# An order by a list scheduler, with gelus in place in PSUM, for a long-convolution and expert-layer kernel

## The chip, the cores and the metric

The kernel runs on one core of a Trainium2 chip. The core has TensorE (PE, its weight loads shown as PEld), VectorE (DVE), ScalarE (ACT), GpSimd (POOL) and SyncE (SP), each with an instruction queue of its own that runs in order; SP only issues transfers here. Products are written to PSUM, eight banks of 128 x 512 words of 32 bits; DVE and ACT read and write PSUM, POOL and the transfers do not. The metric is the device time of one execution in microseconds, the median of the runs; lower is better.

## What is computed

A filter along the time axis by a real Fourier transform of 3008 points, for 8 batches of 256 channels, and then, for each of the 24064 tokens, two products with a gelu between them:

```python
X = np.fft.rfft(x, axis=1)                       # x: (8, 3008, 256)
y = np.fft.irfft(X * (filt_r + 1j * filt_i)[None], n=3008, axis=1)
h = y.reshape(8 * 3008, 256) @ w_in              # 256 -> 2048
g = h * (1.0 / (1.0 + np.exp(-1.702 * h)))
out = (g @ w_out).astype(np.float32)             # 2048 -> 256
```

## The kernel before

The transform is split into 64 x 47 points. `fft(b)` is the way into and out of the frequencies. Its first step takes six tiles of x (512 KB each), splits every half tile into a high part (ACT, line 406) and a rest (POOL, line 407), multiplies both with a table (three matmuls into one bank, `mm3`), splits the result again (lines 411, 412) and stores it in the scratch array a_d by four transfers per tile, issued by ACT (line 417). Its second step runs for i = 0 to 15: `forward` multiplies a piece of a_d, loaded into zy by POOL's queue (line 426), with a table, joins the halves (`halves`, a copy on ACT, line 393, and an addition on DVE, line 394), applies the filter (`product`, lines 384 to 386 on DVE, 387 on POOL) and splits the result (lines 457, 458); `backward` multiplies it back, joins halves, and stores pairs of results in b_d by ACT (line 473). `pair_signal` (lines 499 on) loads four pieces of b_d (br), does the last inverse step on PE (lines 493, 495) for two tiles of 512 tokens and forms sums and differences of them on DVE (line 544), split again by ACT and POOL (lines 537 to 547).

Numbers are 32 bits wide. Every factor is held as a high part and a rest in the matmul's own 32-bit format (F32R), so that one product is three matmuls.

From batch 1 on, the expert layer works on two tiles of tokens (t = 0, 1) and two blocks of 128 hidden features (f = 0, 1) together, by seven products in place of eight, whose combination leaves the four results c_f,t. One such round is a *cycle*: 21 matmuls of the first layer (`product_of`, line 756, weights wt from a ring of three slots that line 174 loads from w_1) and 24 of the second layer for the cycle before (`second_of`, line 778, weights from a second ring of three loaded from w_2). A batch is three u (pairs of tiles; the last pair has 512 and 448 tokens) of eight cycles: 24 cycles, and batches 1 to 7 make 168. In a cycle the bank pa gathers four products one after the other; after the first, second and third, ACT copies its state to SBUF (e, lines 814, 823, 827). pb and pg each have a product of their own and get a copy added by DVE (lines 817, 829, 838); the sum goes to SBUF (c_s), except that pg gets one more product after line 829 has read it. The gelu runs twice on ACT (line 763 to the high part gh, line 764 in full width to SBUF) and the rest gl is the difference of the two (line 765, on POOL for two of the four results and on DVE for the other two).

Four of the eight PSUM banks (ps_h) serve pa, pb, pg and all products of the fft and the inverse transform, and four (ps_o) the sums of the second layer. While batch b is in the expert layer, `tick` advances fft(b+1) in 48 steps over the first 82 of 96 quarter cycles. The order in each engine's queue, the buffers and the semaphores are set by the framework's scheduler with a timing model of its own. Batch 0 runs in another form of the same layer (`mlp`).

Of the kernel before, what the change touches and what calls it, by code (L numbers as in the profile page):

```python
# [142 lines left out]

@with_exitstack
def tile_kernel(
# [9 lines left out]
    nc = tc.nc  # L155
# [7 lines left out]
    def raw(name):  # L163
        return sb.tile([P, 4, D], F32, tag="raw", name=name, bufs=7)

    def half(name):
        return sb.tile([P, 2, D], F32R, tag="half", name=name, bufs=4)

# [227 lines left out]
    def fft(b):  # L396

        a_d = dram.tile([2, 48, 64, D], F32, tag="a_d", name=f"a_d{b}")
        for c in range(6):
            xr = raw(f"x_{b}_{c}")  # L400
            load_in(xr, x[b, c])
            ah, al = (sb.tile([P, 4, D], F32R, tag="raw", name=f"a{n}_{b}_{c}", bufs=7) for n in "hl")
            for u in range(2):
                xh, xl = half(f"xh_{b}_{c}_{u}"), half(f"xl_{b}_{c}_{u}")
                src = xr[:, 2 * u : 2 * u + 2, :]
                nc.scalar.copy(xh, src)  # L406
                nc.gpsimd.tensor_tensor(xl, src, xh.bitcast(F32), ALU.subtract)  # L407
                ps = ps_h.tile([P, 2, D], F32, tag="h", name=f"s1_{b}_{c}_{u}")
# [4 lines left out]
                yield  # L413
            for j in range(2):
                n = NH * j + 4 * c
                for k, a in enumerate((ah, al)):
                    nc.scalar.dma_start(
                        a_d[k, n : n + 4].rearrange("n k d -> k n d"), a[64 * j : 64 * j + 64].bitcast(F32)
                    )
# [15 lines left out]
        def second(i, m, src, name):  # L435

            ps = [ps_h.tile([P, 2, D], F32, tag="h", name=f"{name}_{b}_{i}_{k}") for k in range(2)]
# [26 lines left out]
        def backward(i):  # L464
            g, u = divmod(i, 2)
            if u == 0:
                bes[g] = raw(f"b_{b}_{g}")
            ps = second(i, 2, zy[0][:Q, 2 + i % 2], "i2")
            halves(ps, bes[g][:Q, 2 * u : 2 * u + 2, :])
            if u == 1:  # L470
                be = bes.pop(g)
                for k in range(2):
                    nc.scalar.dma_start(b_d[:, 32 * k + 4 * g : 32 * k + 4 * g + 4, :], be[64 * k : 64 * k + 48])
# [5 lines left out]
        for i in range(2):  # L479
            yield  # L480
        for i in range(17):
            if i < 16:
                forward(i)
                yield
            if i:
                backward(i - 1)
                yield
# [26 lines left out]
    def pair_signal(b, u, ops):  # L514
# [10 lines left out]
        for k, t in enumerate((2 * u, 2 * u + 1)):  # L525
# [5 lines left out]
            for m in range(2):  # L531
                ps = ps_h.tile([P, 512], F32, tag="h", name=f"i1_{b}_{t}_{m}")
# [17 lines left out]
    def finish(pos, w, at, name):  # L550

        o = sb.tile([P, 2, 512], F32, tag="out", name=name)
# [173 lines left out]

    wa = const.tile([P, 4096], F32R, tag="wi_0", name="wa")
    wb = const.tile([P, 4096], F32R, tag="wi_1", name="wb")
    wc = const.tile([P, 4096], F32R, tag="wo_0", name="wc")
    c_f = const.tile([P, 2, 512], F32, tag="tab", name="c_f")  # L730
    ring_1 = [a.rearrange("p (h a c) -> p h a c", h=2, a=7) for a in (wa[:, 0:1792], wa[:, 1792:3584], wb[:, 0:1792])]
    ring_2 = [wc[:, 1024 * i : 1024 * i + 1024].rearrange("p (i h d) -> p i h d", i=2, h=2) for i in range(3)]
    g_h = [wb[:, 2048 + 512 * i : 2560 + 512 * i] for i in range(2)] + [wc[:, 3072:3584]]
    g_l = [wb[:, 3072 + 512 * i : 3584 + 512 * i] for i in range(2)] + [wc[:, 3584:4096]]
    g_h += [sb.tile([P, 512], F32R, tag="gh", name=f"ph{i}") for i in range(2)]
    g_l += [sb.tile([P, 512], F32R, tag="gl", name=f"pl{i}") for i in range(2)]
    c_s = [c_f[:, i] for i in range(2)] + [sb.tile([P, 512], F32, tag="g", name=f"pc{i}") for i in range(2)]
    turn = {"h": 0, "l": 0, "c": 0}
# [5 lines left out]
    def load_1(c):  # L744
        load_in(ring_1[c % 3].bitcast(F32), w_1[c % CYCLES])

    def load_2(c):
        load_in(ring_2[c % 3].bitcast(F32), w_2[c % CYCLES])

    def temp(name):  # L750
        return sb.tile([P, 2, D], F32, tag="half", name=name, bufs=4).rearrange("p a d -> p (a d)")

    def product_of(ps, c, a, y, w, first):
        wt = ring_1[c % 3]
# [5 lines left out]
    def gelu(src, w, cs, on):  # L760
# [3 lines left out]
        nc.scalar.activation(cs[:, :w], src[:, :w], AF.Gelu_apprx_sigmoid)  # L764
        on.tensor_tensor(gl[:, :w], cs[:, :w], gh[:, :w].bitcast(F32), ALU.subtract)  # L765
        return gh, gl

    def second_of(z, k):
# [5 lines left out]
        gp, w, wt = gs[f, t], ws[t], ring_2[c % 3]  # L774
        first, last = c % CYCLES == 0 and k < 2, c % CYCLES == CYCLES - 1 and k > 1
        for n, (wk, gk) in enumerate(((0, 0), (1, 0), (0, 1))):
            for m in range(2):
# [3 lines left out]
                )  # L781
# [102 lines left out]
```

## Time and profile before

| | us |
|---|---|
| median of 3 runs (lowest, highest) | 2706.75 (2699.62, 2708.13) |
| the profiled execution | 2708.51 |
| its span, first to last instruction | 2706.6 |

Busy time in that span: PE 2447.3 us (90%), PEld 1910.5 (71%), DVE 1845.9 (68%), ACT 1638.6 (61%), POOL 1478.1 (55%). The granted clock of PE has a mean of 0.967. Time runs through batch 0 to 437 us, batches 1 to 7 start at about 437, 765, 1098, 1436, 1771, 2108 and 2446 us, counted by the first copy of line 814 in each. In the views by stretch the columns are the stretch, its length, the busy time of PE, PEld, DVE, ACT and POOL with the number of instructions, the granted clock, the DMA share and GB/s. In the rows below times are microseconds unless marked ns; "<-" before a name says what ended a wait; a tile is named without its buffer number. Matmuls overlap, so PE's busy time counts the stretches in which at least one of them is under way.

### The profile page before, as it was taken

The page shows a single profiled execution, that of the slowest core. Times are in us where ns is not written, and L with a number is a line of the kernel's source. Part 1 is how long each engine was busy: PE and PEld are TensorE (multiplying, and loading weights), DVE is VectorE, ACT ScalarE, POOL GpSimd, SP SyncE. Part 2 cuts the span into 40 slices and gives each one's busy share as a digit, 9 for nine tenths or more (in the row PEclk, how much of TensorE's full clock was granted, in tenths as well). Part 3 has the DMA queues.
Part 4 walks back from the last instruction along what each step waited for, and adds up shares of the span by engine and source line. Part 5 has one row for each costly group of instructions (what it writes and reads, how often), then busy time and mean ns, then how long its engine had stood idle before and what let it go on. Part 6 is the DMA issues. An engine that isn't in the chain of part 4 may idle for free. (4 is left out here: it accounts for less than half of the span.)

```text
span 2706.6 us, 32274 instructions
## 1 busy us (share of the span) xinstructions
PE 2447.3 (90%) x10578; PEld 1910.5 (71%) x10578; DVE 1845.9 (68%) x2435; ACT 1638.6 (61%) x2937; POOL 1478.1 (55%) x1149
## 2 busy tenths in 40 slices
PE   7898899888998889989899898998889989899999
PEld 6666678666776667766677666776667766678887
DVE  6767984488745886559865598645886459965443
ACT  5555555566655666656666566655666656666665
POOL 3654643477545774447645476544774447754232
PEclk9899999899999999989999999999999989999999
DMA  9454446686667856668566676676866667655443
GB/s 264 146 159 124 122 116 205 175 209 181 201 217 191 214 169 206 224 179 214 160 202 229 179 209 179 187 226 179 210 180 190 222 181 207 187 174 170 158 146 106
DMA packets 199191, 500.49 MB, mean 185 GB/s; under 512 B 21488, under 2 KB 94448, under 8 KB 199024
## 3 DMA queue, kind: packets, MB, share of 16 engines
q1 hardware_dynamic: 120640, 387.50, 46.5%
q0 software_dynamic: 25088, 44.05, 8.6%
q10 hardware_dynamic: 53296, 66.86, 8.4%
q8 instruction: 85, 1.39, 0.2%
q14 instruction: 82, 0.67, 0.1%
HBM read 392.95 MB, written 105.38 MB: 184 GB/s over the span
## 5 line engine op out<-in xcount | busy, mean ns | idle before, releaser
L778 PE MATMUL o<-wb,wc 128*128 128x512 f32 (+1 forms) x1620 | 443.1, 397 | 31.1 <-POOL wb L765 16.1
L458 POOL TENSOR_TENSOR zy<-c_buf,zy 48x512 fp32r<-48x512 f32 x224 | 333.3, 1488 | 92.4 <-DVE zy L457 80.8
L778 PEld LDWEIGHTS o<-wb,wc 128*128 128x128 f32 x1620 | 303.6, 191 | 111.0 <-POOL wb L765 23.5
L387 POOL TENSOR_TENSOR c_buf<-c_buf,u_buf 112x512 f32<-112x512 f32 x128 | 187.7, 1466 | 241.0 <-DVE c_buf L386 240.6
L778 PE MATMUL o<-ph,wc 128*128 128x512 f32 (+1 forms) x1072 | 296.4, 396 | 5.4 <-ACT ph L763 3.9
L829 DVE TENSOR_TENSOR c_f<-g,e 128x512 f32<-128x512 f32 (+1 forms) x168 | 112.2, 668 | 260.7 <-ACT e L827 235.5
L765 POOL TENSOR_TENSOR wb<-c_f,wb 128x512 fp32r<-128x512 f32 (+1 forms) x135 | 179.2, 1327 | 188.3 <-ACT c_f L764 109.5
L765 POOL TENSOR_TENSOR pl<-c_f,ph 128x512 fp32r<-128x512 f32 (+1 forms) x135 | 181.5, 1345 | 178.9 <-ACT c_f L764 92.9
L778 PEld LDWEIGHTS o<-ph,wc 128*128 128x128 f32 x1072 | 203.8, 192 | 53.3 <-ACT ph L763 11.4
L778 PE MATMUL o<-wc 128*128 128x512 f32 (+1 forms) x804 | 226.1, 398 | 10.5 <-POOL wc L765 6.1
L764 ACT ACTIVATE c_f<-c_f 128x512 f32<-128x512 f32 x336 | 208.2, 623 | 14.7 <-DMA br<-b_d 7.0
L426 POOL DMA_DIRECT2D zy<-a_d x224 | 128.7, 576 | 140.6 <-DMA a_d<-al 66.3
L827 ACT COPY e<-a 128x512 f32<-128x512 f32 (+1 forms) x168 | 95.5, 569 | 154.8 <-PE a L756 153.3
L778 PE MATMUL o<-pl,wc 128*128 128x512 f32 (+1 forms) x536 | 170.9, 397 | 19.1 <-POOL pl L765 11.2
L778 PEld LDWEIGHTS o<-wc 128*128 128x128 f32 x804 | 151.8, 192 | 49.4 <-POOL wc L765 9.9
L838 DVE TENSOR_TENSOR pc<-g,e 128x512 f32<-128x512 f32 x168 | 115.6, 688 | 99.3 <-PE g L756 96.7
L394 DVE TENSOR_TENSOR c_buf<-s,c_buf 48x512 f32<-48x512 f32 x224 | 154.0, 687 | 34.7 <-ACT c_buf L393 30.1
L394 DVE TENSOR_TENSOR b<-i,b 48x512 f32<-48x512 f32 x224 | 153.9, 687 | 27.2 <-ACT b L393 22.1
L407 POOL TENSOR_TENSOR xl<-x,xh 128x512 fp32r<-128x512 f32 x84 | 114.6, 1365 | 103.0 <-ACT xh L406 81.1
L765 DVE TENSOR_TENSOR wb<-pc,wb 128x512 fp32r<-128x512 f32 (+1 forms) x135 | 126.3, 936 | 60.0 <-ACT pc L764 59.2
L457 DVE CAST zy<-c_buf 48x512 fp32r<-48x512 f32 x224 | 144.0, 643 | 26.0 <-POOL c_buf L387 21.6
L765 DVE TENSOR_TENSOR pl<-pc,ph 128x512 fp32r<-128x512 f32 (+1 forms) x133 | 121.9, 917 | 57.9 <-ACT pc L764 57.0
(172 smaller groups left out, 5904.1 us busy)
## 6 DMA issues: line engine op xcount, KB each, us to landing
wa<-w SPq DMA_DIRECT2D x112, 896.0 KB, 5.7
wc<-w SPq DMA_DIRECT2D x168, 512.0 KB, 3.5
wb<-w SPq DMA_DIRECT2D x56, 896.0 KB, 6.2
f_buf<-fs SPq DMA_DIRECT2D x224, 192.0 KB, 3.8
zy<-a_d POOLq DMA_DIRECT2D x224, 192.0 KB, 4.5
x<-in_x_dram SPq DMA_DIRECT2D x48, 512.0 KB, 4.3
a_d<-ah ACTq DMA_DIRECT2D x84, 256.0 KB, 4.3
a_d<-al ACTq DMA_DIRECT2D x84, 256.0 KB, 4.6
```

Of the source, the lines that this page charges most:

```text
L387: nc.gpsimd.tensor_tensor(u1, u1, u2, ALU.add)
L394: nc.vector.tensor_tensor(dst[h], ps[k][h], dst[h], ALU.add)
L407: nc.gpsimd.tensor_tensor(xl, src, xh.bitcast(F32), ALU.subtract)
L426: nc.gpsimd.dma_start(zy[0][64 * k : 64 * k + 48, i % 2].rearrange("p k s d -> p k (s d)"), src.rearrange("n k s d -> n k (s d)"),)
L457: nc.vector.tensor_copy(y[h, k], u1[h])
L458: nc.gpsimd.tensor_tensor(y[o, k], u1[h], y[h, k].bitcast(F32), ALU.subtract)
L764: nc.scalar.activation(cs[:, :w], src[:, :w], AF.Gelu_apprx_sigmoid)
L765: on.tensor_tensor(gl[:, :w], cs[:, :w], gh[:, :w].bitcast(F32), ALU.subtract)
L778: nc.tensor.matmul(pos[t][m][:, :w], wt[:, f, wk, P * m : P * m + P], gp[gk][:, :w], start=first and n == 0, stop=last and n == 2,)
L827: nc.scalar.copy(e[3][:, :w1], pa[:, :w1])
L829: nc.vector.tensor_tensor(cs[:, :w1], pg[:, :w1], e[3][:, :w1], ALU.add)
L838: nc.vector.tensor_tensor(cs, pg, e[2], ALU.add)
```

## The change

From batch 1 on the kernel no longer leaves the order to the framework. Engine calls are recorded with a price each (`Planner.add`, `price`), with the accesses that they depend on; then `plan` runs a list schedule over them and issues them in the order of its start times, under the framework's manual mode. A matmul's due time is its place in program order on PE, other steps are due as late as those that need them allow; each engine takes the ready step with the earliest due time, PE nothing that is due more than 30 us later than its head. The schedule also picks the slot of each temporary tile and the PSUM bank, holds SBUF-only steps of DVE and all steps of POOL apart, and prices a transfer by its size in one shared pipe. Besides the order:

- The additions of pb and of the second pg are written to the PSUM bank itself, and the second gelu is written over its source (PSUM for three of the four results); the difference reads it there. POOL takes one difference of four, DVE three. The first addition of pg still goes to SBUF.
- Rings of w_1 and w_2 have two slots instead of three, and gh and gl four instead of five each. The load of w_1 for cycle c+1 is recorded at the start of cycle c, that of w_2 for cycle c in cycle c.
- Ten buffers of 4 KB per partition are split into pools: two for x, four for the split results and b, four for the rest (there were seven in one pool). x is loaded one tile further ahead.
- All transfers go through SP: the stores of a_d and b_d from ACT, the loads of zy from POOL.
- The fft's parts are paced by PE's time (weights at the `yield`s) so that they end 36 us ahead of the batch's end. Batch 0's stores are all issued ahead of the new part.

```diff
+    def price(self, eng, call, args, aps):
...
+            return (0.6 if eng == "gpsimd" else 0.4), 3.2 + whole / 280e3, False
...
+                return (n + 32) / 2400, 0.1, False
...
+            return 0.18 + n * (0.8e-3 if any(spaces) else 0.88e-3), 0.0, False
...
+                return 0.15 + n * 1.06e-3, 0.0, False
+            fast = call in ("tensor_copy", "memset")
+            return 0.15 + n * (0.54e-3 if fast else 1.06e-3), 0.0, True
+        return 0.15 + n * 2.25e-3, 0.0, True
...
+                elif eng == "tensor" and target[n] > here + self.REACH:
+                    pass
+                else:
+                    key = (target[n] if eng == "tensor" else o.due, n)
+                    if (best is None or key < best[0]) and room(o, t):
...
+        store = nc.sync if nc.on else nc.scalar
...
-                nc.gpsimd.dma_start(
-                    zy[0][64 * k : 64 * k + 48, i % 2].rearrange("p k s d -> p k (s d)"),
+                (nc.sync if nc.on else nc.gpsimd).dma_start(
+                    zy[0][64 * k : 64 * k + 48, i % 2].rearrange("p k s d -> p k (s d)").bitcast(F32 if nc.on else F32R),
...
+    while stores:
+        store()
+    ctx.enter_context(tc.manual_schedule())
+    nc.on = True
...
+    ring_1 = [wa[:, 1792 * i : 1792 * i + 1792].rearrange("p (h a c) -> p h a c", h=2, a=7) for i in range(2)]
+    ring_2 = [wc[:, 1024 * i : 1024 * i + 1024].rearrange("p (i h d) -> p i h d", i=2, h=2) for i in range(2)]
...
+    for name, i, j in (("x", 0, 2), ("ab", 2, 6), ("raw", 6, 10)):
+        nc.pool(name, raws[i:j])
...
-        nc.scalar.activation(cs[:, :w], src[:, :w], AF.Gelu_apprx_sigmoid)
-        on.tensor_tensor(gl[:, :w], cs[:, :w], gh[:, :w].bitcast(F32), ALU.subtract)
+        nc.scalar.activation(src[:, :w], src[:, :w], AF.Gelu_apprx_sigmoid)
+        on.tensor_tensor(gl[:, :w], src[:, :w], gh[:, :w].bitcast(F32), ALU.subtract)
...
+    SPAN = 3 * CYCLES * 45 * 544 / 2400
+    TAIL, PARTS = 36.0, 6.0 + 12 * 1.5 + 2 * 5.0 + 32 * 3.3
...
-        if c + 2 < len(cycles):
-            load_1(c + 2)
-        if c == 0:
-            load_2(0)
         if c + 1 < len(cycles):
-            load_2(c + 1)
+            load_1(c + 1)
+        load_2(c)
...
-                cs = of(c_s, "c")
-                nc.vector.tensor_tensor(cs, pb, e[1], ALU.add)
-                gs[0, 0] = gelu(cs, 512, cs, nc.gpsimd)
+                nc.vector.tensor_tensor(pb, pb, e, ALU.add)
...
+            if k == 0:
+                gs[0, 0] = gelu(pb, 512, nc.vector)
             if k == 3:
                 product_of(pg, c, 2, t4, 512, False)
-                cs = of(c_s, "c")
-                nc.vector.tensor_tensor(cs, pg, e[2], ALU.add)
-                gs[1, 0] = gelu(cs, 512, cs, nc.vector)
+                nc.vector.tensor_tensor(pg, pg, e2, ALU.add)
+                gs[1, 0] = gelu(pg, 512, nc.vector)
```

## Rows read from the trace of the kernel before

**Rows 1.** Batches 3, 7: length, engines busy (count), clock, DMA share, GB/s.

```profile
1098.20:1436.40 338.20, 304.98 (x1280) 233.70 (x1280) 237.04 (x306) 208.42 (x372) 195.02 (x154) 0.96 0.68 196
...
2445.70:2706.60 260.90, 254.67 (x1164) 213.72 (x1164) 112.75 (x148) 159.19 (x287) 84.38 (x59) 1.00 0.43 143
```

**Rows 2.** The same columns in four stretches of batch 3.

```profile
1098.20:1224.50 126.30, 111.58 (x455) 85.40 (x456) 64.16 (x83) 73.22 (x134) 59.47 (x47) 0.93 0.69 207
...
1224.50:1343.30 118.80, 104.45 (x422) 76.24 (x422) 105.59 (x135) 75.32 (x131) 83.09 (x70) 0.97 0.70 187
...
1343.30:1436.40 93.10, 88.95 (x405) 72.07 (x403) 67.28 (x90) 59.88 (x110) 52.46 (x39) 1.00 0.62 192
...
1210.70:1251.70 41.00, 34.62 (x136) 23.60 (x135) 38.65 (x51) 26.80 (x48) 27.62 (x24) 1.00 0.86 211
```

**Rows 3.** The chain that ended last: start us, us, what.

```profile
2600.95 2.27 PE o L778 x10
...
2611.15 2.27 PE o L778 x10
...
2649.77 1.37 PE g L756 x6
...
2659.56 1.37 PE g L756 x6
```

**Rows 4.** Order of time, PE: start us, us, engine, line, operation, count.

```profile
465.83 1.05 PE L493 MATMUL i<-t_sb,br 128*128 128x128 f32 x8
```

**Rows 5.** Waits in batch 3: waiter <- releaser, us in all, times, longest.

```profile
DVE c_f L829 <- ACT e L827: 33.0, 8, 9.1
...
PEld g L756 <- DVE c_f L829: 13.7, 10, 3.8
```

**Rows 6.** Waits of SP's own queue over the whole span, same columns.

```profile
SPq L174 <- PE o L778: 708.4, 121, 14.3
```

**Rows 7.** Groups by line: count, busy us, mean ns, idle before.

```profile
L838 DVE TENSOR_TENSOR pc<-g,e 128x512 f32<-128x512 f32 x168 | 115.6, 688 | 99.3 <-PE g L756 96.7
...
L765 DVE TENSOR_TENSOR wb<-pc,wb 128x512 fp32r<-128x512 f32 (+1 forms) x135 | 126.3, 936 | 60.0 <-ACT pc L764 59.2
...
L544 DVE TENSOR_TENSOR t<-y,t 128x512 f32<-128x512 f32 x42 | 74.9, 1784 | 0.5
...
L764 ACT ACTIVATE pc<-pc 128x512 f32<-128x512 f32 x168 | 106.7, 635 | 6.3 <-DVE b L394 1.3 <-ACT wb L763 0.8 <-ACT ph L763 0.6
...
L764 ACT ACTIVATE pc<-a 128x512 f32<-128x512 f32 (+1 forms) x168 | 96.8, 576 | 0.0
```

**Rows 8.** One line's durations: ns min/median/max.

```profile
L544 DVE TENSOR_TENSOR t<-y,t x42: 678/1762/3240, 430.4 to 2578.5; 128x512 f32<-128x512 f32 x42
```

**Rows 9.** Order of time, ACT and its queue, in batch 3.

```profile
1130.90 2.11 ACTq L417 DMA_DIRECT2D a_d<-al  x2
...
1133.05 0.62 ACT L406 CAST xh<-x 128x512 fp32r<-128x512 f32 x1 [2.24 <-DMA a_d<-ah]
```

**Rows 10.** Batch 3: queues (packets, MB, share), issues (median us to landing).

```profile
q10 hardware_dynamic: 7552, 9.44, 9.7%
...
q0 software_dynamic: 3584, 6.29, 9.7%
...
wa<-w SPq DMA_DIRECT2D x16, 896.0 KB, 5.5
```

**Rows 11.** Issues in 1210 to 1250 us, same columns.

```profile
br<-b_d SPq DMA_DIRECT2D x4, 256.0 KB, 12.6
...
wb<-w SPq DMA_DIRECT2D x1, 896.0 KB, 10.5
```

**Rows 12.** Order of time around the start of batch 1.

```profile
433.40 0.86 PE L756 MATMUL a<-y_a,wa 128*128 128x512 f32 x3
...
436.96 0.58 ACT L814 COPY e<-a 128x512 f32<-128x512 f32 x1
...
441.50 0.58 SPq L600 DMA_DIRECT2D out_dram<-out  x1
```

More of the change, by code (lines that the diff above doesn't have):

```diff
@@ L144, in tile_kernel, with __init__, __getattr__, issue @@
+class Stream:
+    def __init__(self, planner, name, real):
+        self.planner, self.name, self.real = planner, name, real
+    def __getattr__(self, call):
+        real, planner = getattr(self.real, call), self.planner
+        def issue(*args, **kw):
+            if planner.on:
+                return planner.add(self.name, call, args, kw)
+            return real(*args, **kw)
+        return issue
 @with_exitstack
@@ L435, in second @@
         def second(i, m, src, name):
-            ps = [ps_h.tile([P, 2, D], F32, tag="h", name=f"{name}_{b}_{i}_{k}") for k in range(2)]
+            ps = [held(f"{name}_{b}_{i}_{k}") for k in range(2)]
             for k in range(2):
@@ L732, in tile_kernel @@
[L732 to L737, printed above, removed]
@@ L738, in tile_kernel, with fill @@
-    turn = {"h": 0, "l": 0, "c": 0}
+    def fill(tag, n, size, dtype, bufs):
+        return [sb.tile([P, size], dtype, tag=tag, name=f"{tag}_{i}", bufs=bufs) for i in range(n)]
+    ring_1 = [wa[:, 1792 * i : 1792 * i + 1792].rearrange("p (h a c) -> p h a c", h=2, a=7) for i in range(2)]
+    ring_2 = [wc[:, 1024 * i : 1024 * i + 1024].rearrange("p (i h d) -> p i h d", i=2, h=2) for i in range(2)]
+    g_h = [wc[:, 2048 + 512 * i : 2560 + 512 * i] for i in range(2)] + fill("gh", 2, 512, F32R, 2)
@@ new lines, in tile_kernel @@
+    g_l = [wc[:, 3072 + 512 * i : 3584 + 512 * i] for i in range(2)] + fill("gl", 2, 512, F32R, 2)
+    nc.pool("c", [c_f[:, i] for i in range(2)])
+    nc.pool("e", fill("g", 2, 512, F32, 2) + [wb[:, 3072 + 512 * i : 3584 + 512 * i] for i in range(2)])
+    raws = fill("raw", 7, 1024, F32, 7) + [wb[:, 1024 * i : 1024 * i + 1024] for i in range(3)]
+    for name, i, j in (("x", 0, 2), ("ab", 2, 6), ("raw", 6, 10)):
+        nc.pool(name, raws[i:j])
+    nc.pool("half", fill("half", 4, 512, F32R, 4) + [wa[:, 3584:4096]])
@@ L740, in of @@
+    nc.pool("out", fill("out", 2, 1024, F32, 2))
+    nc.pool("h", [ps_h.tile([P, 512], F32, tag="h", name=f"bank_h{i}") for i in range(4)])
+    nc.pool("o", [ps_o.tile([P, 512], F32, tag="o", name=f"bank_o{i}") for i in range(4)])
+    turn = {"h": 0, "l": 0}
     def of(ring, kind):
@@ L781, in second_of, with advance @@
                 )
+            advance(2 * (w + 32) / 2400)
         if last:
             finish(pos[t], w, at + 512 * t, f"{name}_{t}")
+    SPAN = 3 * CYCLES * 45 * 544 / 2400
+    TAIL, PARTS = 36.0, 6.0 + 12 * 1.5 + 2 * 5.0 + 32 * 3.3
+    clock, due, part = [0.0], [0.0], [iter(())]
+    def advance(us):
+        clock[0] += us
+        while due[0] <= clock[0]:
+            w = next(part[0], None)
+            due[0] = 1e9 if w is None else due[0] + w * (SPAN - TAIL) / PARTS
     prev, sig = None, None
     cycles = [(b, u, p) for b in range(1, B) for u in range(3) for p in range(CYCLES)]
-    for c in range(2):
-        load_1(c)
+    load_1(0)
     for c, (b, u, p) in enumerate(cycles):
         if u == 0 and p == 0:
-            next_batch(b, 0)
+            if b + 1 < B:
+                part[0], due[0] = fft(b + 1), clock[0]
         if p == 0:
@@ L794, in tile_kernel @@
             ws = (512, 512 if u < 2 else 448)
-            pos = [[ps_o.tile([P, 512], F32, tag="o", name=f"o_{b}_{u}_{t}_{m}") for m in range(2)] for t in range(2)]
+            pos = [
+                [nc.tile("o", (P, 512), F32, f"o_{b}_{u}_{t}_{m}") for m in range(2)]
+                for t in range(2)
+            ]
             y11, y21 = ([op["b"][:, h, m] for h in range(2)] for m in range(2))
@@ L855, in tile_kernel @@
     store()
+    nc.on = False
+    nc.plan()
 _OUTS = [((P, 2, B * S), "float32")]
```

311 lines of the change are left out of this document (270 added, 41 removed).

## The prediction

> **What bounds the kernel now.** I read the views in this order: the busy shares of a batch, of four stretches inside it, the chain that ended last, the waits, and the durations of the steps that the change touches.
>
> PE is busy for 305 of the 338.2 us of batch 3 [rows 1], but a busy PE is not a full one, so I price its work. In the last batch nothing but the mixture layer (products, gelus, second products; 24 cycles of 45 matmuls) and two inverse transforms runs. There the same point of a cycle returns after 10.20 us, 0.2267 us a matmul of 512 columns, or after 9.79 us in the third u, where a part is 448 wide [rows 3]. 16 x 10.20 + 8 x 9.79 = 241.5 us for the cycles of a batch. Batches 1 to 6 also carry the next batch's fft (96 matmuls of 0.2267 us are 21.8 us, 8 small ones at most 1 us) and the inverse transforms (96 records, of which 8 take 1.05 us [rows 4], 12 us). Sum: 276 us. Measured, batch 3 takes 338.2 us [rows 1], and the mean of batches 1 to 6 is 334.8 us, (2445.70 - 436.96)/6, from the first copy of batch 1 [rows 12] to the start of the last batch [rows 1]. So some 60 us in each of six batches are PE standing or at its lower clock: the granted clock is 0.96 there, a mix of its two levels, 1.2 and 2.4 GHz, and 1.00 in the last batch, where PE hardly stands [rows 1]. That batch has little left to win: 241.5 us, 24 second products of the batch before (5.4 us) and 64 inverse records (8.4 us) are 255 of its 260.9 us.
>
> Where do the 60 us lie? At 276/1280 = 0.2156 us for a mean matmul, batch 3's first 126.3 us hold 455 matmuls, 98 us of work (78%), the next 118.8 us hold 91 us (77%), the last 93.1 us hold 87 us (94%) [rows 2]. In the first stretch DVE and ACT are half idle: there the order stands in its own way, no engine does. In the middle DVE is tight, 38.65 of 41 us [rows 2]. The waits agree: DVE's largest is line 829's addition for the copy of line 827 (33.0 us), and PE's weight loads wait 13.7 us for that addition [rows 5]. It lies in a loop PE, ACT, DVE, PE, with 15 matmuls in program order between the product that starts it and the one that needs its bank, some 3.4 us, and each engine on the way has other work queued ahead.
>
> **The change part by part.** *The order.* It adds no work on PE and is worth what it takes back of the 60 us. I take the best that these rows show for a stretch with everything in it, 94%: 276/0.94 = 293 us a batch. Bounds: 276 us (nothing stands) and 335 us (nothing won). Gain: 6 x (335 - 293), about 250 us. DVE, ACT and the transfers have to fit into 293 us:
>
> *DVE.* The additions stay at about 0.69 us, that of line 838, which reads PSUM [rows 7]; written to PSUM they are in no row, and I take the same. A third subtraction per cycle comes over from POOL: 24 x 0.69 = +16.5 us a batch. The two that DVE has read SBUF twice and average 0.936 us [rows 7]; with the gelu in PSUM they should cost 0.69 as well: 48 x 0.25 = -12 us. DVE: 237 + 4.5, some 242 us of 293, 83%. Below that lies what collisions with POOL cost: line 544's subtraction in SBUF takes 1.784 us on average and 0.678 at the least [rows 7, 8], so six of them a batch give back up to 7 us if the order keeps them apart, and others like them more. Were the subtraction to stay at 0.936 us, DVE would have 260 us, 89%.
>
> *ACT.* The number of copies and gelus stays. A gelu in place (PSUM to PSUM) is in no row; the nearest are PSUM to SBUF, 0.576 us, and SBUF to SBUF, 0.635 [rows 7]. I take the first, since the source decides between these two: four of a cycle's eight gelus change, 24 x 4 x 0.055 = -5 us; at 0.635, nothing. 40 issues of transfers leave ACT's queue. Two of them took it 2.11 us, and ACT stood 2.24 us before its next step [rows 9]; six such groups a batch are 13 us. ACT: about 203 of 293, 69%.
>
> *All transfers from SP.* Per batch 24 stores of a_d, 16 of b_d and 32 loads of zy come to SP, 176 issues in all; at about 0.58 us [rows 12] that is 102 us of 293. Of the bytes, POOL's queue moved 6.29 MB in the engine time in which ACT's moved 9.44 MB, 9.7% of 338 us each [rows 10]; at ACT's rate they cost 22 instead of 33 us. The DMA share becomes (0.68 x 338 - 11)/293 = 75%. The price is order: all that is behind SP's head waits for what the head waits for, and SP stood up to 14.3 us for a buffer [rows 6], which a weight ring three deep covered. The ring becomes two deep: load c+1 starts when cycle c-1 is done and must land within cycle c, 10.2 us of PE time. Its median landing is 5.5 us [rows 10]; behind four loads of br, which took 12.6 us themselves, it was 10.5 us [rows 11]. So I count 0 in most cycles and 1 or 2 us near the three br bursts of a batch; these lie within the 6% that I leave.
>
> The Trainium skill, page "DMA: Bandwidth & Descriptors", section "Queues, rings and completion order", says that each DMA engine takes turns, packet by packet, between the queue rows that have work. This speaks against the change: a weight load on SP's row has its turn beside the bursts of ACT and POOL today, and in a single row it would stand behind them. No row separates the two; the 10.5 us are a load behind others of its own row, which agrees.
>
> *Additions and gelu in PSUM.* The banks of pb and pg are now held through two gelus and the subtraction, 0.6 + 0.6 + 0.69 = 1.9 us longer, that of pa by the subtraction, 0.7 us: 4.5 us more per cycle, on four banks shared with the fft. Bounds: 0 (another bank is free) and 4.5/4 = 1.1 us of PE per cycle. I take 0, since the second products, 24 of 45 matmuls, need none of these banks and can fill. The Trainium skill, page "PSUM — Partial Sum Buffer", section "Summary: rules for kernel authors", asks to evacuate PSUM promptly; by that, the third rival below is the outcome. No run here shows it yet.
>
> *The seam.* The new part's first weight load comes behind batch 0's last store on SP, issued at 441.50 us [rows 12]. With its 0.58 us, as much for the load and 5.5 us of landing, the first product starts near 448 us instead of 433.40, and the first copy near 450 instead of 436.96 [rows 12]: +13 us; 0 if the load is issued ahead of the store.
>
> *Sum*, against the profiled execution's span of 2706.6 us (the execution took 2708.5 us, the median of the three runs is 2706.75, so nothing is scaled): 437 + 13 + 6 x 293 + 260 (the last batch) = 2468 us.
>
> **The rivals.**
> 1. *Near the ideal.* 98%, 282 us a batch: 710 + 6 x 282 = 2402 us. For it: the last batch. Against: no stretch with an fft in it comes close.
> 2. *DVE is the bound of the middle.* The 118.8 us stretch has 8 cycles and 105.6 us of DVE [rows 2], of them 8 x (3 x 0.69 + 2 x 0.93) = 31 us the mixture's and 74 us the rest's. The change paces the fft's second half over about 15.5 instead of 14.1 cycles: 74 x 0.91 + 8 x 6 x 0.69 = 100 us, which at the 94% of the 41 us stretch take 107 us, where PE needs 90/0.94 = 96. 11 us over 8 cycles are some 17 us over the part that the easy ends of a batch don't absorb: 310 us, 2570 us. For it: those 94% are there today. Against: fewer collisions, and the fft may lag into the easy stretch.
> 3. *Banks.* The upper bound above, 24 x 1.1 = 27 us a batch: 320 us, 2630 us.
> 4. *Slower: weights late.* With a ring of two and one queue, the weight load stands at SP behind a store or a zy load that waits for DVE, and lands too late in most cycles. It decides from 710 + 6T > 2707 on, T = 333 us: 40 us over 293, 1.7 us in each cycle, an issue delay plus landing of more than 12 us every time. At 13.5 us T is 341 us and the time 2756 us. For it: 10.5 and 12.6 us [rows 11], SP's 14.3 us [rows 6]. Against: a median of 5.5 us leaves 4.7 us of slack.
> 5. *It doesn't do what it says.* Durations on the chip differ from those that the order was made with, and the engines wait as long in other places: T about 333 us, 2708 us.
>
> **How the numbers follow.** Forecast (T from 286 to 302 us) 0.49, near the ideal 0.12, DVE 0.19, banks 0.08, slower 0.09, no change 0.03. The predicted time is the forecast's. The range takes in the forecast, half of the ideal's cases and the DVE rival, and reaches to the banks: 2380 to 2625 us. A measurement of this kernel tells about 0.3%, 8 us, from no change: faster 0.88, same 0.03, slower 0.09.
>
> **What would show it.** Right: batches 1 to 6 of 286 to 302 us each, a clock of 0.99 or 1.00, DVE near 80% of a batch, its subtraction after a gelu at 0.69 us, no issue of transfers on ACT, PE's waits for DVE's addition below 5 us a batch, the first product of batch 1 near 448 us. DVE rival: middle stretches with DVE at 94%. Banks: PE's weight loads waiting for a subtraction or a gelu. Weights: PE waiting for the transfer of the weights. Wrong would be a mean batch over 325 us, or an in-place gelu far from 0.58 us.

## The result, and the profile after

| | us |
|---|---|
| changed kernel, median of 4 runs (lowest, highest) | 2451.99 (2448.9, 2453.48) |
| kernel before, median of 4 runs | 2704.55 |
| ratio, 95% interval | 0.9066, 0.9047 to 0.9084 |
| span of the profiled execution, before and after | 2706.6, 2447.1 |

The time fell by 9.3%; 2468 us were forecast. In the trace of the changed kernel nearly every line of the planned part is L393, the place where the plan issues its steps, so groups are told apart by tiles: bank_h is a bank of ps_h, bank_o one of ps_o. Batches are counted from the start of DVE's one addition into c_f per cycle (line 829 before), since that step is the same in all variants. By it batches 1 to 6 took (2453.4 - 443.1)/6 = 335.0 us before and (2194.2 - 440.0)/6 = 292.4 us after. Of the 259.5 us between the two spans, 3.1 lie ahead of batch 1, 256.1 in batches 1 to 6, and 0.3 in the last.

The views by stretch of the changed kernel (columns as in [rows 1]): batch 3, its cycles 0 to 7, 8 to 15 and 16 to 23, ten microseconds from its cycle 6, and the last batch:

```profile
1026.20:1320.20 294.00, 284.57 (x1282) 231.26 (x1281) 218.94 (x331) 204.30 (x370) 139.88 (x97) 0.99 0.75 225
...
1026.20:1134.50 108.30, 102.78 (x459) 83.08 (x458) 69.07 (x105) 73.23 (x134) 48.38 (x35) 0.98 0.84 253
...
1134.50:1231.20 96.70, 94.27 (x418) 74.76 (x417) 87.46 (x129) 70.94 (x127) 53.41 (x37) 1.00 0.71 213
...
1231.20:1320.20 89.00, 87.52 (x409) 73.41 (x408) 62.41 (x99) 60.13 (x111) 38.09 (x27) 1.00 0.69 206
...
1100.00:1110.00 10.00, 5.90 (x24) 4.06 (x23) 9.76 (x13) 4.74 (x9) 5.29 (x4) 0.97 0.64 164
...
2194.20:2447.10 252.90, 247.72 (x1136) 208.28 (x1134) 109.20 (x166) 150.49 (x275) 46.83 (x33) 0.99 0.42 148
```

Batch 3 is down from 338.2 us in [rows 1] to 294.0 us with the same 1280 matmuls (a few records at the edges aside) and the clock at 0.99. DVE's busy time fell from 237 to 219 us although it has 24 steps more; ACT's fell by 4 us, POOL's by 55. Of the 44.2 us that the batch lost, 23.8 are time in which PE did nothing (33.2 us before, 9.4 after), and 20.4 are PE's busy time, at a clock of 0.99 in place of 0.96. By the price of the prediction the three stretches are at 91%, 93% and 99%; those of [rows 2] were at 78%, 77% and 94%. More than half of what is left stands in one place, cycles 4 to 7: they take 54.5 us for 206 matmuls, 44.4 us of work by the same price, 10 of the batch's 18 us over it (the row stands under e10 and e11). In the fifth row, ten microseconds of that place, PE has 5.90 us and DVE 9.76.

What PE waits for in batch 3 of the changed kernel, the longest first (waiter, releaser, us in all, times, longest):

```profile
PEld bank_h L393 <- DVE c_f L393: 5.9, 4, 3.9
...
PE bank_h L393 <- DVE c_f L393: 4.5, 3, 3.5
...
PEld bank_h L393 <- DVE c_buf L393: 2.3, 6, 1.0
...
PEld bank_o L393 <- ACT wc L393: 2.0, 4, 0.9
```

The loop through the addition into c_f is still the largest wait, 5.9 us for the weight loads against 13.7 in [rows 5]; waits for a gelu or its difference are 2 us each or less, and nothing on PE waits for a transfer.

The chain through that place, in order of time (start us, us, what):

```profile
1104.93 1.68 DVE u_buf L393
...
1106.63 1.65 DVE u_buf L393
...
1108.34 0.57 issue
...
1108.91 0.69 DVE c_f L393
...
1109.65 2.07 PE bank_h L393 x5
```

The addition that PE needs (c_f) stands on DVE behind two products of the filter (u_buf) that take 1.68 and 1.65 us in place of 0.69, with POOL at work in SBUF beside them. Over the whole span, the 160 of these products that had no step of POOL beside them took at most 0.691 us, the 64 others up to 2.23.

Durations in the changed kernel over the whole span (ns min/median/max, first and last start):

```profile
L393 ACT ACTIVATE bank_h<-bank_h x504: 533/593/627, 438.2 to 2438.0; 128x512 f32<-128x512 f32 x168
...
L393 DVE TENSOR_TENSOR bank_h<-bank_h,g x224: 680/700/700, 436.0 to 2429.5; 128x512 f32<-128x512 f32 x112
...
L393 DVE TENSOR_TENSOR gl<-bank_h,gh x336: 606/691/694, 442.6 to 2438.6; 128x512 fp32r<-128x512 f32 x113, 128x448 fp32r<-128x448 f32 x55
```

The gelu in place takes 593 ns, the addition in place 700, the difference after it 691, with a maximum of 694.

Transfers of batch 3 of the changed kernel (queues, then issues with the median us to landing), to be read beside [rows 10], and the start of the planned part in order of time, beside [rows 12]:

```profile
q1 hardware_dynamic: 25857, 66.01, 74.8%
...
wa<-w SPq DMA_DIRECT2D x24, 896.0 KB, 7.5
...
zy<-a_d SPq DMA_DIRECT2D x32, 192.0 KB, 4.1
```

```profile
405.85 0.82 SPq L393 DMA_DIRECT2D wa<-w  x2
...
429.93 0.86 PE L393 MATMUL bank_h<-y_a,wa 128*128 128x512 f32 x3
...
437.81 0.58 SPq L406 DMA_DIRECT2D out_dram<-out  x1
```

All transfers of the kernel are on one queue now; the weights land after 7.5 us instead of 5.5. The first weights of batch 1 were issued at 405.85 us, 32 us ahead of batch 0's last store, and the first product started at 429.93 us.

### The profile page after: what moved, and what is told of

Its sections match the earlier page's. It is cut to its first block, busy times and chain, and to the rows that moved or that the text cites. A ratio compares the mean times of both kernels' runs of the same rounds, so it can differ in the third digit from the quotient of the medians.

```text
span 2447.1 us, 32185 instructions
## 1 busy us (share of the span) xinstructions
PE 2333.3 (95%) x10578; PEld 1897.0 (78%) x10578; DVE 1751.6 (72%) x2603; ACT 1615.3 (66%) x2937; POOL 1105.8 (45%) x789
## 4 chain that ended last, share of the span: by engine, by line
PE 76%; DVE 15%; DMA 3%; issue 2%; ACT 2%; POOL 1%; SPq 0%; ACTq 0%; DVEq 0%; POOLq 0%
PE bank_h L393 38%; PE bank_o L393 33%; PE h L406 2%; PE o L406 2%; DVE c_buf L393 1%; DVE u_buf L393 1%; DVE gl L406 1%; DVE wb L393 1%; DVE c_buf L406 1%; DVE u_buf L406 1%; DVE w_tu L406 1%; DVE bank_h L393 1%; DVE zy L393 1%; DVE ws L406 1%; DVE gl L393 1%
## 5 line engine op out<-in xcount | busy, mean ns | idle before, releaser
L393 PE MATMUL bank_o<-wc 128*128 128x512 f32 (+1 forms) x2016 | 553.8, 390 | 5.4 <-ACT wc L393 3.5
L393 PE MATMUL bank_h<-y_a,wa 128*128 128x512 f32 (+1 forms) x1584 | 434.9, 393 | 14.8 <-DVE c_f L393 8.8
L393 PEld LDWEIGHTS bank_o<-wc 128*128 128x128 f32 x2016 | 378.2, 189 | 91.0 <-ACT wc L393 10.6
L393 POOL TENSOR_TENSOR wc<-c_f,wc 128x512 fp32r<-128x512 f32 (+1 forms) x168 | 214.0, 1274 | 495.6 <-ACT c_f L393 366.5
L393 PE MATMUL bank_o<-gh,wc 128*128 128x512 f32 (+1 forms) x1344 | 390.2, 388 | 0.5 <-ACT gh L393 0.2
L393 PEld LDWEIGHTS bank_h<-y_a,wa 128*128 128x128 f32 x1584 | 294.0, 189 | 85.1 <-DVE c_f L393 11.8
L393 POOL TENSOR_TENSOR zy<-c_buf,zy 48x512 fp32r<-48x512 f32 x192 | 273.7, 1426 | 132.1 <-DVE zy L393 116.4
L393 DVE TENSOR_TENSOR gl<-bank_h,gh 128x512 fp32r<-128x512 f32 (+1 forms) x336 | 226.8, 677 | 114.5 <-ACT bank_h L393 109.4
L393 ACT ACTIVATE bank_h<-bank_h 128x512 f32<-128x512 f32 (+1 forms) x504 | 297.8, 591 | 0.0
L393 PEld LDWEIGHTS bank_o<-gh,wc 128*128 128x128 f32 x1344 | 251.8, 188 | 49.2 <-ACT gh L393 2.6
L393 ACT COPY wb<-bank_h 128x512 f32<-128x512 f32 (+1 forms) x309 | 178.6, 578 | 161.8 <-PE bank_h L393 159.3
L393 PE MATMUL bank_h<-y_bt,wa 128*128 128x512 f32 (+1 forms) x960 | 272.1, 393 | 13.3 <-DVE c_f L393 10.0
L393 POOL TENSOR_TENSOR c_buf<-c_buf,u_buf 112x512 f32<-112x512 f32 x96 | 125.1, 1303 | 285.4 <-DVE c_buf L393 273.1
L393 ACT ACTIVATE gh<-bank_h 128x512 fp32r<-128x512 f32 (+1 forms) x336 | 197.4, 588 | 67.2 <-DVE bank_h L393 37.6
L393 DVE TENSOR_TENSOR raw<-bank_h,raw 48x512 f32<-48x512 f32 (+1 forms) x264 | 180.8, 687 | 63.0 <-ACT raw L393 55.2
L393 DVE TENSOR_TENSOR bank_h<-bank_h,g 128x512 f32<-128x512 f32 x224 | 155.8, 696 | 93.3 <-PE bank_h L393 50.6
L393 PEld LDWEIGHTS bank_h<-y_bt,wa 128*128 128x128 f32 x960 | 177.9, 189 | 54.6 <-DVE c_f L393 13.5
L393 PE MATMUL bank_o<-gl,wc 128*128 128x512 f32 (+1 forms) x672 | 217.0, 387 | 0.0
L393 ACT COPY g<-bank_h 128x512 f32<-128x512 f32 x224 | 131.8, 588 | 111.0 <-PE bank_h L393 103.5
L393 DVE TENSOR_TENSOR wc<-bank_h,wc 128x512 fp32r<-128x512 f32 x168 | 115.7, 689 | 109.8 <-ACT bank_h L393 108.9
L393 DVE TENSOR_TENSOR c_f<-bank_h,wb 128x512 f32<-128x512 f32 (+1 forms) x168 | 112.2, 668 | 78.7 <-ACT wb L393 76.2
L393 PE MATMUL bank_h<-zy,de_sb 112*112 112x512 f32 (+1 forms) x408 | 154.6, 392 | 10.6 <-DVE wc L393 6.4
```

Of the source, the lines that this page charges most:

```text
L393: getattr(getattr(self.nc, o.eng), o.call)(*map(real, o.args), **{k: real(v) for k, v in o.kw.items()})
```

## The experiments

My theory: the order carries the gain; the gelus in place and the single queue each add little. The rivals give it to one of those two. A second question is what the remaining 18 us of batch 3 over the priced 276 are: late transfers, DVE as the bound, or the order itself. All ratios are to the kernel before on the same chip, by 3 rounds each.

| variant | median us | ratio (95%) | batch, us (mean of 1 to 6) |
|---|---|---|---|
| changed kernel | 2452.0 | 0.9066 (0.9047, 0.9084) | 292.4 |
| e3 order undone | 2689.0 | 0.9973 (0.9950, 0.9995) | 331.0 |
| e1 issuing undone | 2490.5 | 0.9240 (0.9215, 0.9264) | 299.2 |
| e2 in place undone | 2515.6 | 0.9332 (0.9307, 0.9357) | 303.1 |
| e7 before, all from SP | 2665.3 | 0.9897 (0.9877, 0.9918) | 328.3 |
| e8 before, in place | 2661.3 | 0.9836 (0.9786, 0.9887) | 327.6 |
| e9 another plan | 2460.9 | 0.9143 (0.9119, 0.9167) | 294.3 |
| e4 SBUF steps not kept apart | 2474.4 | 0.9179 (0.9149, 0.9209) | 297.0 |
| e5 few weights, planned anew | 2399.5 | 0.8908 (0.8890, 0.8926) | 283.9 |
| e6 less DVE, planned anew | 2397.8 | 0.8902 (0.8884, 0.8919) | 284.1 |
| e10 few weights, same plan | 2449.7 | 0.9054 (0.9011, 0.9097) | 292.4 |
| e11 less DVE, same plan | 2420.9 | 0.8946 (0.8896, 0.8997) | 287.4 |
| e12 the fft earlier and slower | 2401.7 | 0.8876 (0.8835, 0.8918) | 284.3 |

**e3, the order alone undone.**

```diff
-    ctx.enter_context(tc.manual_schedule())
```

> The changed kernel with its planner's choice of buffers, banks and recorded program, but the framework's own scheduler (as before the change) sets the order of each engine's queue. Theory (the order carries the gain): batches 1 to 6 go back from 294 to 330 us or more, time 2670 to 2800 us, and PE again waits for DVE's addition into c_f. Rival (gelus in place and transfers from SP carry it): at most 310 us a batch, 2450 to 2550 us.

The gain is gone: 0.9973, 331.0 us a batch. Its batch 3, and three of its waits there:

```profile
1103.90:1436.70 332.80, 301.07 (x1281) 233.01 (x1280) 230.02 (x331) 203.75 (x370) 139.61 (x97) 0.97 0.66 199
```

```profile
PEld bank_h L393 <- ACT wb L393: 8.2, 12, 2.7
...
PEld bank_h L393 <- DVE c_f L393: 6.8, 9, 4.1
...
PEld bank_o L393 <- ACT wc L393: 6.1, 5, 2.8
```

With the same steps, banks and queues as the changed kernel, 332.8 us instead of 294.0, and PE stands in many places for a few microseconds each, six kinds of wait of 5 to 8 us among its weight loads (three are shown), at a clock of 0.97. The theory's lower bound for a batch, 330 us, is met. The buffers here were chosen for another order, so 331 us is not what the old order does at its best; e7 and e8 bound that.

**e7 and e8, one other part alone, in the kernel before.**

```diff
-                    nc.scalar.dma_start(
+                    nc.sync.dma_start(
...
-                nc.gpsimd.dma_start(
+                nc.sync.dma_start(
...
-                    nc.scalar.dma_start(b_d
+                    nc.sync.dma_start(b_d
```

> The kernel before with one part of the change alone: all its transfers from SP, the order still the framework's. Theory (the order carries the gain, this part nothing by itself): 2660 to 2760 us. Rival (the stalls came from transfers issued on ACT): below 2620 us. Second rival (one queue makes the weights late): above 2780 us.

```diff
-                nc.vector.tensor_tensor(cs, pb, e[1], ALU.add)
-                gs[0, 0] = gelu(cs, 512, cs, nc.gpsimd)
+                nc.vector.tensor_tensor(pb, pb, e[1], ALU.add)
+                gs[0, 0] = gelu(pb, 512, pb, nc.vector)
...
-                gs[0, 1] = gelu(pa, w1, of(c_s, "c"), nc.vector)
+                gs[0, 1] = gelu(pa, w1, pa, nc.vector)
...
-                nc.vector.tensor_tensor(cs, pg, e[2], ALU.add)
-                gs[1, 0] = gelu(cs, 512, cs, nc.vector)
+                nc.vector.tensor_tensor(pg, pg, e[2], ALU.add)
+                gs[1, 0] = gelu(pg, 512, pg, nc.vector)
```

> The kernel before with one part of the change alone: additions and second gelus in place in PSUM, three of the four differences on DVE; order and issuing as before. Theory (the order carries the gain): the banks are held longer and the framework's order knows nothing of collisions, 2640 to 2740 us. Rival (in place carries the gain): below 2600 us. Rival on banks: above 2760 us.

Both lie within the times that the theory gave, though e7's theory gave its part nothing by itself, and both are a small gain: 1.0% for the queue, 1.6% for the gelus in place. In e9 below two plans with the same steps differ by 0.85%, so what each of the two is worth alone stays uncertain. Together with e3: without the new order none of the gain is left, so the order is worth most of the 9.3%, some 7% if the other two are taken off in full. No run has the new order with both other parts undone.

**e1 and e2, one other part undone, under the new order.**

```diff
-        store = nc.sync if nc.on else nc.scalar
+        store = nc.scalar
...
-                (nc.sync if nc.on else nc.gpsimd).dma_start(
+                nc.gpsimd.dma_start(
...
-                    (nc.sync if nc.on else nc.scalar).dma_start(b_d
+                    nc.scalar.dma_start(b_d
```

> Undoes one part: in the planned part the stores of a_d and b_d are issued by ACT again and the loads of zy by POOL. Theory (order carries the gain): the plan knows of the issues, ACT has 70% and POOL less than 50% of work, so 0 to 4 us a batch, 2450 to 2476 us. Rival (the queues were the stall): 10 us a batch or more, above 2510 us. Second rival (one queue delays the weights): faster, below 2440 us, and the weights' median landing falls from 7.5 us back towards 5.5 us.

299.2 us a batch, and 1.9% more time than the changed kernel: between the theory's bound and the rival's. The plan prices an issue on ACT at 0.4 us; what they took in e1's trace (ns min/median/max):

```profile
L393 ACTq DMA_DIRECT2D a_d<-raw x144: 582/630/1875, 451.3 to 1991.1; - x144
...
L393 ACTq DMA_DIRECT2D b_d<-raw x96: 308/309/318, 552.9 to 2198.2; - x96
```

24 stores of a_d a batch at 0.63 us, some at 1.9, stand in ACT's queue, and 32 loads in POOL's, whose busy time in batch 3 is 157 us instead of 140. Which of the two costs the 1.9% isn't shown: the order is another one too, and the longest waits of PE's weight loads in batch 3 name neither, but DVE's steps into raw (6.7 us) and its difference (5.6 us). The Trainium skill, page "DMA: Bandwidth & Descriptors", section "Issuing engines are not separate DMA queues", says that issuing from several engines saves only the sequencer's time to issue, which it calls usually small beside the transfer. The row agrees, 0.63 us beside a median landing of 5.9 us. That such issues cost the kernel something where a compute engine's queue makes them is argued from the 1.9%. The second rival, that one queue makes the weights late, falls: their median landing was 7.3 us with three queues and 7.5 us with one.

```diff
-                nc.vector.tensor_tensor(pb, pb, e, ALU.add)
+                nc.vector.tensor_tensor(cs0, pb, e, ALU.add)
...
-                gs[0, 1] = gelu(pa, w1, nc.vector)
+                gs[0, 1] = gelu(pa, w1, nc.vector, nc.tile("c", (P, 512), F32, f"c1_{name}"))
...
-                gs[0, 0] = gelu(pb, 512, nc.vector)
+                gs[0, 0] = gelu(cs0, 512, nc.gpsimd)
...
-                nc.vector.tensor_tensor(pg, pg, e2, ALU.add)
-                gs[1, 0] = gelu(pg, 512, nc.vector)
+                nc.vector.tensor_tensor(cs, pg, e2, ALU.add)
+                gs[1, 0] = gelu(cs, 512, nc.vector)
```

> Undoes one part: additions and second gelus go to SBUF again as before the change, one more difference is POOL's again; four slots for them (one taken from the copies e, which keep three). Theory: DVE's reads of two SBUF operands collide with POOL, whose order the plan keeps apart, so it costs a few us a batch: 2455 to 2500 us. Rival (in place carries the gain): above 2540 us. Rival on banks (holding them costs): below 2440 us.

303.1 us a batch, and 2.9% more time: more than I gave it, less than the rival needs. Its batch 3, the difference read from SBUF (ns min/median/max), and the longest wait of PE's weight loads in batch 3:

```profile
1051.30:1354.20 302.90, 288.26 (x1282) 230.43 (x1281) 226.40 (x306) 211.37 (x370) 182.91 (x121) 0.99 0.73 219
```

```profile
L393 DVE TENSOR_TENSOR gl<-c_f,gh x157: 606/687/2821, 453.3 to 2505.3; 128x512 fp32r<-128x512 f32 x137, 128x448 fp32r<-128x448 f32 x20
```

```profile
PEld bank_o L393 <- DVE gl L393: 8.3, 6, 3.7
```

With 24 steps fewer DVE is busier than in the changed kernel, 226 against 219 us: a difference that takes 0.69 us at its median takes up to 2.82 us beside POOL, where the one that reads PSUM never exceeds 0.694. Of the 157 here, the 43 with no step of POOL beside them took at most 0.694 us; of the 336 in the changed kernel 233 had a step of POOL beside them and were no slower for it. The second product waits for this difference, 8.3 us in batch 3; batch 3 of the changed kernel has no such wait. POOL has 183 us instead of 140, since one more difference is its own again, so the 2.9% are the price of the whole part and not of the reads alone. The rival on banks falls: holding them longer costs less than this.

**e9, how much is the plan's luck.**

```diff
-    HOP, REACH, NEAR = 0.2, 30.0, 2.5
+    HOP, REACH, NEAR = 0.22, 30.0, 2.5
```

> The changed kernel with the plan's price of a hand-over between engines at 0.22 instead of 0.20 us: no step changes, only the order that the plan comes to. It measures how much the time depends on the plan's luck. If plans of the same quality agree, within 8 us of 2452 us; if small changes of the plan move the time by 1 to 2%, differences of that size between the other variants say little of the part that they undo.

No step differs, and the ratio is 0.9143 in place of 0.9066: 0.85%, some 21 us, or 9 us by the two medians, which stand beside different runs of the kernel before. Either is more than the 8 us that I gave to plans of the same quality. One other plan doesn't bound the scatter, but differences of this size say nothing of a part. e1 is twice and e2 over three times that.

**e4, the rule that keeps DVE and POOL apart.**

```diff
-            return 0.15 + n * (0.54e-3 if fast else 1.06e-3), 0.0, True
-        return 0.15 + n * 2.25e-3, 0.0, True
+            return 0.15 + n * (0.54e-3 if fast else 1.06e-3), 0.0, False
+        return 0.15 + n * 2.25e-3, 0.0, False
```

> The changed kernel with the plan's rule off that keeps DVE's steps in SBUF and POOL's steps apart; nothing else changes. Theory (collisions are part of what the old order lost): DVE's busy time of a batch rises from 219 us by 10 to 25 us, the difference in PSUM stays at 0.69 us, and the time rises by 3 to 10 us a batch: 2470 to 2515 us. Rival (collisions are hidden): within 8 us of 2452 us.

Two groups of DVE over its whole span (busy us, mean ns of one | idle time before them and what ended it):

```profile
L393 DVE CAST zy<-c_buf 48x512 fp32r<-48x512 f32 x192 | 103.8, 540 | 4.9 <-POOL c_buf L393 0.8
...
L393 DVE TENSOR_TENSOR u_buf<-c_buf,f_buf 48x512 f32<-48x512 f32 x96 | 91.6, 954 | 3.1
```

The cast takes 540 ns on average against 446 in the changed kernel, the product 954 against 791. DVE's busy time of batch 3 is 227 us against 219, less of a rise than the 10 us that I gave as the least, and the time lies 1.25% above: as the theory has it in direction and size, but hardly beyond the luck of e9. It stays open how much of the gain this rule is.

**e5 and e6, two suspects taken out and planned anew.**

```diff
     def load_1(c):
-        load_in(ring_1[c % 2].bitcast(F32), w_1[c % CYCLES])
+        if c < 2:
+            load_in(ring_1[c % 2].bitcast(F32), w_1[c % CYCLES])
...
     def load_2(c):
-        load_in(ring_2[c % 2].bitcast(F32), w_2[c % CYCLES])
+        if c < 2:
+            load_in(ring_2[c % 2].bitcast(F32), w_2[c % CYCLES])
```

> Leaves out all loads of the two weight rings after cycle 1 of the planned part, so the cycles reuse the first two cycles' weights: half of the bytes of a batch go. Theory (in the changed kernel the transfers fill the first 60 us of a batch, share 1.0, so the fft's second half starts some 25 us late and then crowds DVE and PE around 100 us): batches 1 to 6 fall from 294 to 280 to 288 us, time 2360 to 2420 us, and the stretch of cycles 4 to 8 falls from 54 us to 48 to 50 us. Rival (that stretch is DVE's own load): 294 us a batch as before, 2440 to 2455 us.

```diff
-        nc.vector.scalar_tensor_tensor(u2[0:48], xs[64:Q], -1.0, f_i[64:Q], ALU.mult, ALU.mult)
-        nc.vector.tensor_tensor(u2[64:Q], xs[0:48], f_i[0:48], ALU.mult)
+        if not nc.on:
+            nc.vector.scalar_tensor_tensor(u2[0:48], xs[64:Q], -1.0, f_i[64:Q], ALU.mult, ALU.mult)
+            nc.vector.tensor_tensor(u2[64:Q], xs[0:48], f_i[0:48], ALU.mult)
```

> Leaves out two of DVE's steps per filtered pair in the planned part (the two products with the filter's imaginary part), 32 steps and about 26 us of DVE a batch; POOL adds what stands in the buffer from batch 0. Theory (DVE at 75% of a batch is not the bound, only crowded around 100 us): 2 to 8 us a batch, 2400 to 2440 us. Rival (DVE is the bound of the middle): more than 10 us a batch, below 2390 us.

Each takes 8 us off a batch, e5 as its theory has it, e6 a little more than its theory and less than its rival; and cycles 4 to 7 of e5's batch 3 fell from 54.5 us to 44.9, further than the 48 to 50 us that I gave. Taken alone, e5 seemed to show that transfers are late at the start of a batch. But both kernels have another plan, so the next two leave the plan as it is.

**e10 and e11, the same suspects taken out of the same plan.**

```diff
+        loads = 0
         for n in order:
             o = ops[n]
+            if o.call == "dma_start" and any(k.startswith(("w_1", "w_2")) for k in o.names):
+                loads += 1
+                if loads > 4:
+                    continue
```

> The changed kernel's own plan, but the loads of the weight rings after the first two cycles are left out as the plan is issued; the order of all other steps stays. Theory (late transfers at the start of a batch upset the order that the plan has chosen): cycles 4 to 8 fall from 54 us to 46 to 50 us, a batch from 294 to 284 to 290 us, 2400 to 2435 us. Rival (the crowding stands in the order itself): 2440 us or more.

```diff
         for n in order:
             o = ops[n]
+            if o.eng == "vector" and o.args[0].tensor.name.startswith("u_buf"):
+                continue
```

> The changed kernel's own plan, but two of DVE's steps per filtered pair (the products with the filter's imaginary part, 32 a batch, 26 us) are left out as it is issued; the order of the rest stays. Theory (DVE delays PE only where it is crowded): 3 to 8 us a batch, 2400 to 2435 us. Rival 1 (DVE bounds the middle): below 2390 us. Rival 2 (what a new plan without these steps gained was the plan's luck): 2440 us or more.

Cycles 4 to 7 of batch 3, from the addition into c_f of cycle 4 to that of cycle 8 (the expectations call them cycles 4 to 8), in the changed kernel, in e10 and in e11:

```profile
1080.00:1134.50 54.50, 48.98 (x206) 37.92 (x205) 38.92 (x59) 34.20 (x62) 23.60 (x17) 0.97 0.76 201
```

```profile
1082.40:1137.00 54.60, 49.14 (x205) 37.91 (x204) 38.87 (x59) 34.13 (x62) 23.56 (x17) 0.97 0.42 94
```

```profile
1074.10:1124.00 49.90, 47.56 (x206) 36.88 (x205) 32.00 (x50) 34.03 (x62) 23.49 (x17) 1.00 0.85 221
```

e10 contradicts the theory. With the DMA share at 0.42 instead of 0.76 in this stretch it still takes 54.6 us, and the kernel 2450 us. So transfers that are late on the chip delay nothing there: the place is crowded because the order says so. In e11 the same stretch takes 49.9 us, with the clock at 1.00, and the batch 287.7 us: 4.6 of the 6.3 us saved come from this one place. DVE delays PE where the order crowds it, not as the bound of a batch; the theory for e11 is borne out, and the "bound" of the rival isn't met.

Both together make this reading: the fft's first step has its transfers at a batch's start, the plan prices them in one pipe, and so puts the second step late and then dense. That this is the plan's own price of transfers at work is argued and not shown: in e5 the transfers and their price are both gone, in e10 the transfers alone, and only e5 gains. But every new plan has its own luck, as e9 shows, and e6's new plan too gained more than e11 did in the old one.

**e12, a version that draws on it.** The first step of the fft starts three cycles earlier, in the last cycles of the batch before, and is spread out.

```diff
-                yield 1.5
+                yield 2.5
...
-            due[0] = 1e9 if w is None else due[0] + w * (SPAN - TAIL) / PARTS
+            due[0] = 1e9 if w is None else due[0] + w * stretch[0] / PARTS
...
-        if u == 0 and p == 0:
-            if b + 1 < B:
-                part[0], due[0] = fft(b + 1), clock[0]
+        if c == 0:
+            part[0], due[0] = fft(2), clock[0]
+        if u == 2 and p == 5 and b + 2 < B:
+            part[0], due[0], stretch[0] = fft(b + 2), clock[0], SPAN - TAIL + 30.6
```

> A version that may beat both: the fft of batch b+2 starts in the last three cycles of batch b instead of at the start of batch b+1, and its first step is paced 2.5 instead of 1.5, so that its transfers spread into a stretch where the transfers have room. All arithmetic as in the changed kernel. Theory (transfers at the start of a batch are what is left of the stalls): batches 2 to 6 at 285 to 289 us, 2405 to 2430 us, no 10 us slice with a DMA share of 1.0. Rival (DVE is the bound): 2440 us or more.

2401.7 us, a little better than forecast, 2.1% below the changed kernel and 11.2% below the kernel before, computing all that they do. Batch 1, which has the old start, takes 293.3 us, batches 2 to 6 take 278.5 to 289.0; batches 3 and 4:

```profile
1014.60:1303.60 289.00, 284.01 (x1287) 233.29 (x1286) 221.72 (x331) 204.40 (x372) 140.21 (x98) 0.99 0.75 231
...
1303.60:1583.80 280.20, 279.01 (x1277) 230.49 (x1276) 214.61 (x330) 202.97 (x370) 137.58 (x97) 1.00 0.76 237
```

PE is busy for 279.01 of 280.20 us in batch 4. The batches differ by up to 10 us, so there is luck in it too, and the spread of the transfers isn't its only cause: that no slice of 10 us would be full I had wrong, batch 3 of it begins with 30 us at a DMA share near 1.0. The start and the pace changed together, in a new plan; which of them gains is not shown.

## Why the prediction was right, and where it was not

*The order.* 293 us a batch were forecast from the 94% of the one easy stretch; 292.4 us were measured. e3 shows that the order carries it. That the value came so close has luck in it: e9's plan gives 294.3, and the 94% are a mean of 91, 93 and 99%, not a steady rate. The 94% themselves were read too high. They price all matmuls alike, but 129 of that stretch's 405 are 448 wide; by [rows 3] such a one costs some 0.203 us, and priced by kind, as an estimate, the stretch of [rows 2] stood at 92%, which would have given 300 us a batch. The new order did better than the best stretch before: by the same count its three stretches are at 92, 94 and 97%.

*DVE.* The step that failed is the term of collisions. I had 242 us a batch, counted only what the differences give back, and left the rest out of the sum, with up to 7 us at line 544 named; 219 us were measured. Added up one by one, the durations of DVE's steps in batch 3 lie 49 us above the shortest of their kind in the kernel before and 15 us above it in the changed one; e3, with the steps in PSUM but the framework's order, has 26 us. The difference after the gelu is 0.69 us as forecast. DVE is busy for 74% of a batch, with 9.76 of 10 us where it is crowded: of the rival "DVE is the bound of the middle" the mechanism is found, but not the place or the size. The crowded place is in the first stretch, and in the middle one DVE is busy for 90% and PE's work stands at 93%.

*ACT.* Forecast 203 us, measured 204; the gelu in place 0.59 us against 0.58 (the 0.576 of [rows 7] has narrower steps in it; at 512 columns the two are alike). I counted the issues as 13 us of ACT's order, hidden; e1 prices the issuing on ACT and POOL together at 7 us a batch of the whole, with the luck of another plan in it.

*SP.* The DMA share was forecast at 75% and is 0.75. The weights' landing rose from 5.5 to 7.5 us, which still lies within the 10.2 us of a cycle: nothing on PE waits for a transfer. The rival "weights late" did not come, and e1 shows that the rise isn't the single queue's. With it falls the burst of stores and zy loads that holds up the weights in a shared row: 7.3 against 7.5 us is all that it makes to have those in rows of their own. That was the effect for which I weighed the Trainium skill, page "DMA: Bandwidth & Descriptors", section "Queues, rings and completion order"; no run here shows it.

*Banks.* Counted at 0; in batch 3 of the changed kernel none of PE's waits for a difference is over 2 us in all, and e2, which frees the banks earlier, is slower. The rule of the Trainium skill, page "PSUM — Partial Sum Buffer", section "Summary: rules for kernel authors", to evacuate promptly, didn't decide here: undoing the part costs more than the held banks. Held banks aren't free in every order, though: in batch 3 of e1 and of e3 PE's weight loads wait 5.6 and 6.0 us for a difference that frees one.

*The seam.* This step failed, by 16 us: +13 forecast, -3.1 measured. I had the new part's first load behind batch 0's last store on SP; the framework issued it 32 us ahead of that store, as it had done before the change (409.31 against 441.50 us), so the bound of 0 was the better guess. This is 16 of the 21 us between the sum of 2468 and the span of 2447.1 for which it stood; the six batches make 4 and the last one 1. The load of the kernel before (start us, us, engine, line, operation):

```profile
409.31 0.82 SPq L174 DMA_DIRECT2D wa<-w  x2
```

*PE's waits for the addition.* Below 5 us a batch were forecast; the weight loads waited 5.9 us, 4.5 of them in the one crowded place, and the 4.5 us of the matmuls' own waits lie beside these, not on top of them.

## What to carry to other kernels

Where no engine is full and the waits are spread over many pairs, price the bound engine's work, and take the best stretch that the kernel already has as a first guess of the rate that a better order can reach, pricing its work by kind. A change of the order changes everything behind it: test a suspect inside a fixed order as well as in a new one, and measure one plan that differs by next to nothing to see how much is luck. Where another engine's work in SBUF stretches a step, one operand in an accumulator bank can be worth more than the step's usual duration says. Moving the issue of transfers out of busy engines' queues gained 1.0% and 1.9% here, though by which way stays open.

## What was not expected of the hardware

A DVE step with two SBUF operands took up to 2.82 us beside POOL, four times its 0.69 us, while the same step with one operand in PSUM stayed within 0.606 to 0.694 us in 336 cases, 233 of them with a step of POOL beside them. An ACT gelu of 512 columns from PSUM to PSUM took 594 ns at its median, no less than the 592 ns from PSUM to SBUF in the kernel before. And half of the bytes of a batch could be left out with nothing gained, at a DMA share of 0.75, with 50 us of batch 3 near 1.0.
